# Soft mixture of experts behind linear attention: w2 units 3 and 4 in two loads, six output chunks in a row and their store in two transfers

## The chip and the metric

The kernel runs on one core of one Trainium2 chip. The metric is the time of one execution on the device, in microseconds (us); lower is better.

## What is computed

Linear attention over 8 batches of 8 heads gives a matrix `x` of 4608 tokens by 512, and a soft mixture of 8 experts with 4 slots each works on it:

```python
kv = np.einsum('bhsd,bhse->bhde', k, v)
out = np.einsum('bhsd,bhde->bhse', q, kv)
x = out / sqrt(mean(out * out, -1) + 1e-06) * g_norm      # reshaped to (4608, 512)
...
logits = x @ phi                                           # (4608, 32)
d = softmax of logits over the tokens                      # dispatch
slot_input = (d.T @ x).reshape(E, S_per_e, D)
for e in range(E):
    h = np.maximum(slot_input[e] @ w1[e], 0.0)             # w1[e]: 512 x 1024
    slot_out[e] = h @ w2[e]                                # w2[e]: 1024 x 512
c = softmax of logits over the 32 slots                    # combine
return c @ slot_out                                        # (4608, 512)
```

All of it is float32. The weights are 2 x 8 x 2 MB, the attention's inputs 28 MB, the output 9.4 MB.

## The kernel before

The program is written as one list of operations by hand. A small class (`Order`, with the helper at line 209 that issues all of them) finds out which operation must wait for which and puts a semaphore there; every engine works in the order of the program. So all rows of the profile name line 209, and operations are told apart by their tiles. SBUF is one `arena` of 160 places of 1 KB a partition that inputs, weights and output chunks use one after another; `W_AT` (lines 35 to 39) and `OUT_AT` (line 52) say who lies where.

The first part, to about 113 us, streams k, v and q in, forms the attention's output tile by tile, its norm, the logits and the dispatch sums. Weights follow the inputs on the same queue, SP's; a load waits only until the last reader of its place is done. The rows of `W_ROWS` (lines 40 to 51) are the weights' transfers in the order of the queue; a row with two entries is one transfer.

The second part is the experts. `expert_h(e)` multiplies by w1, `expert_y(e, hf)` by one half (256 columns) of w2: 8 matmuls, 16 passes in float32. The experts from 2 on have w2 in another form: `w2_unit` (line 841) puts the first halves of experts 2 and 3 in unit 2, of 4 and 5 in unit 3, of 6 and 7 in unit 4, and the second halves in units 5, 6 and 7. So the first half of the output columns needs units 0 to 4 only. Unit 3 goes to place 72 and unit 4 behind it to place 88, in one transfer of 128 rows of 32 KB:

```python
    (("w2", 3, None), ("w2", 4, None)),
    (("w2", 5, None), ("w2", 6, None)),
    (("w2", 7, None),),
```

When all first halves are summed, `gather(0)` and `mix(0)` copy and rearrange the result, and `output(0, k, f)` makes chunks 0 to 5 of the output, 768 KB each: matmuls with the combine weights into PSUM, a copy of one half by ACT and of the other by DVE into the arena (chunks 5 and 11 split DVE's half over both). Three PSUM buffers take turns in the first half; the second half has a fourth. Before, four chunks are made, then the second halves of experts 2 to 5, then chunks 4 and 5, then experts 6 and 7, and `gather(1)`, `mix(1)` and chunks 6 to 11 follow. `fill_wide` issues matmuls that nobody reads; two of them stand where PE waits for units 3 and 4 (line 984).

Stores go out when their last chunk is copied. `store_apart` (line 902) sends the odd rows of chunk 0 in four small transfers (two of them from GpSimd) that use a few of the 16 DMA engines each; `store_first` (line 915) sends the even rows of chunks 0 to 2 in one transfer of 64 rows and the odd rows of chunks 1 and 2 in another; then come chunks 3 to 5, 6 and 7, and 8 to 11 in one transfer each (`OUT_ROWS`, line 53).

Of the kernel before, what the change touches and what calls it, by code (L numbers as in the profile page):

```python
# [23 lines left out]
NCH = NT // CT  # L24
NX = 14
EARLY = (5, 1, 0)
LATE_FILL = (4, 3, 3, 1, 1, 2)
TOK = 4608
UNIT = 4096
KB = 256  # L30
# [14 lines left out]
    (("w1", 5, None),),  # L45
    (("w2", 2, 0), ("w1", 6, None)),
    (("w1", 7, None),),
    (("w2", 3, None), ("w2", 4, None)),
    (("w2", 5, None), ("w2", 6, None)),
    (("w2", 7, None),),  # L50
)
OUT_AT = (32, 38, 44, 104, 110, 116, 122, 128, 134, 140, 146, 152)
OUT_ROWS = ((0, 1, 2), (3, 4, 5), (6, 7), (8, 9, 10, 11))
CHUNK = 4 * 12 * 32
APART = (("gpsimd", 0, 26, 2, 1), ("gpsimd", 41, 11, 2, 2), ("sync", 26, 15, 5, 1), ("sync", 52, 12, 3, 1))
STEPS = (7, 6)
# [221 lines left out]
def soft_moe_linear_attention(nc, first_in, kv_in, q0_in, q1_in, kv4_in, kv5_in, t3_in, w_in, out):  # L278
# [37 lines left out]
    def load_w(kind, u, part=None):  # L316
        i = [row[0] for row in W_ROWS].index((kind, u, part))
        lo = sum(row_length(row) for row in W_ROWS[:i])
        n = row_length(W_ROWS[i])
        src = w_in[:, lo * P : (lo + n) * P].rearrange("o (p n) -> (o p) n", p=P)  # L320
        t = homes(kind, u)[part or 0]
        if n > t.shape[-1]:
            t = place(W_AT[kind, u][part or 0], n)
        nc.sync.dma_start(t, src)
# [522 lines left out]
    def expert_h(e):  # L847
        ph = ps.tile([P, 2, 512], F32, tag="m", name=f"ph{e}")[:, 0, :256]
        for c in range(4):
            for j in range(4):  # L850
                nc.tensor.matmul(
                    ph[32 * j : 32 * j + 32],
                    lhsT=sTe[:, (4 * e + c) * NS : (4 * e + c + 1) * NS],
                    rhs=w_block("w1", e, 4 * c + j),
                    start=c == 0,
                    stop=c == 3,
                )
        h = wk.tile([P, 256], F32, tag="part", name=f"h{e}", bufs=3)
        nc.scalar.activation(h, ph, AF.Relu, scale=rs)

        x = xts[(NT - 1 - e // 2) % NX].rearrange("p j n -> p (j n)")
        hTs[e] = x[:, e % 2 * 256 : e % 2 * 256 + 256].rearrange("p (c n) -> p c n", n=NS)
        nc.vector.transpose(out=hTs[e].rearrange("p c n -> p (c n)"), in_=h)
# [51 lines left out]
    def store_first():  # L915
        at = 64 * CHUNK
        for i in range(2):
            n = (3 - i) * CHUNK
            nc.sync.dma_start(out[:, at : at + 64 * n].rearrange("o (m n) -> (o m) n", n=n), place(OUT_AT[i], n)[i::2])
            at += 64 * n  # L920

    def output(hf, k, f):
        z = zs[hf]
        n = (hf * NCH + k) * 2 + f
        at = OUT_AT[n]
        st = place(at, 4 * CT * NS).rearrange("p (a n) -> p a n", a=4)
        shared = n in SHARED
        for v in range(2):
            fourth = hf == 1 and (2 * n + v) % 4 == 3
            apart = shared and v == 1  # L930
            pots = [
                ps.tile([P, 2, 512], F32, tag="y" if y else "m", name=f"po{hf}_{k}_{f}_{v}_{i}", bufs=1 if y else None)
                for i, y in enumerate((False, fourth) if apart else (fourth,))
            ]
            for u in range(2):
                lo = 32 * (2 * v + u)
                po = pots[u if apart else 0]
                nc.tensor.matmul(
                    po[:, 0 if apart else u, : CT * NS].rearrange("p (g x) -> p g x", g=2),
                    lhsT=z[f][lo : lo + 32],  # L940
                    rhs=cT[k][lo : lo + 32],
                    start=True,
                    stop=True,
                )
            if apart:
                nc.vector.tensor_copy(out=st[:, 2], in_=pots[0][:, 0, : CT * NS])
                nc.scalar.copy(st[:, 3], pots[1][:, 0, : CT * NS])
            elif v == 0:
                nc.scalar.copy(st[:, 0:2], pots[0][:, :, : CT * NS])
            else:  # L950
                nc.vector.tensor_copy(out=st[:, 2:4], in_=pots[0][:, :, : CT * NS])
        if n == 0:
            store_apart()
        if n == 2:
            store_first()
        for row in OUT_ROWS[1:]:
            if row[-1] == n:
                lo, m = row[0] * 4 * CT * NS, len(row) * 4 * CT * NS
                nc.sync.dma_start(
                    out[:, lo * P : (lo + m) * P].rearrange("o (p n) -> (o p) n", p=P), place(OUT_AT[row[0]], m)  # L960
                )

    step_over(STEPS[0])
    expert_h(0)
    expert_h(1)
    load_w("w2", 3)
    expert_y(0, 0)
    combine(0)
    expert_h(2)
# [11 lines left out]
    expert_y(3, 0)  # L981
    expert_y(0, 1)
    expert_y(1, 1)
    fill_wide(ps.tile([P, 2, 512], F32, tag="m", name="fill")[:, 0], LATE_FILL[5])
    for e in range(4, NE):
        expert_y(e, 0)
    chunks = [(k, f) for k in range(NCH) for f in range(2)]
    gather(0)
    mix(0)
    output(0, *chunks[0])  # L990
    output(0, *chunks[1])
    output(0, *chunks[2])
    output(0, *chunks[3])
    expert_y(2, 1)
    expert_y(3, 1)
    expert_y(4, 1)
    expert_y(5, 1)
    output(0, *chunks[4])
    output(0, *chunks[5])
    expert_y(6, 1)  # L1000
    expert_y(7, 1)
    gather(1)
# [87 lines left out]
```

## Time and profile before

| | us |
|---|---|
| median of 3 runs | 172.40 (172.13 to 172.85) |
| the profiled execution, its own time | 172.14 |
| its span, from the first to the last instruction | 170.8 |
| PE busy | 150.2 (88%) |
| ACT, DVE, POOL busy | 88.9, 86.0, 59.9 |
| DMA queue of SP | 71.15 MB, 97.6% of 16 engines' span |

The profile covers one execution. A page of it gives busy times and the busy tenths of each engine in 40 slices of the span; a busy PE is one with a matmul in it, whatever that matmul is for. The DMA share of a stretch is the mean over the 16 DMA engines and can pass 1.00 a little, since packets overlap at their ends. "SPq" is SP's queue: its rows give the issue of a transfer, not its run, and the time to landing is counted from the issue to the last of its 16 completions.

### The profile page before, as it was taken

The numbers are of one execution on the slowest core, as the hardware profiler recorded it, in microseconds if no ns is written. First come the engines' busy times: TensorE is split into PE (matmuls) and PEld (weight loads), VectorE is DVE, ScalarE is ACT, GpSimd is POOL, SyncE is SP. The second block draws the span as 40 slices with busy tenths as digits, with TensorE's granted clock in tenths as the row PEclk, the third lists the DMA queues.
The fourth block names the chain that finished last, engine by engine and source line by source line (L and its number), as shares of the span: only waits on it lengthen the run. The fifth ranks groups of instructions, "written<-read, shape, count | busy, mean of one in ns | idle before, by whom it ended". The sixth has DMA issues, their size and how long they took to land.

```text
span 170.8 us, 4512 instructions
## 1 busy us (share of the span) xinstructions
PE 150.2 (88%) x1975; PEld 108.4 (63%) x1975; DVE 86.0 (50%) x184; ACT 88.9 (52%) x230; POOL 59.9 (35%) x72
## 2 busy tenths in 40 slices
PE   7988897989999899999899998999999988989500
PEld 3467776979788888898797785355565453545200
DVE  1122156284677266762946698824888017136600
ACT  3037575796975886859759864202224016146500
POOL 6000708548357745467382679500000004000000
PEclk9999999999999999999999999999999999999955
DMA  5999999999999999999999999999999999999996
GB/s 188 416 433 421 440 421 433 475 415 471 440 410 421 431 440 441 407 403 462 403 453 418 437 405 430 430 435 416 445 453 418 439 410 414 405 426 423 433 437 282
DMA packets 4295, 71.67 MB, mean 420 GB/s; under 512 B 883, under 2 KB 883, under 8 KB 947
## 3 DMA queue, kind: packets, MB, share of 16 engines
q1 hardware_dynamic: 3795, 71.15, 97.6%
q8 instruction: 15, 0.25, 0.5%
q0 software_dynamic: 480, 0.23, 0.5%
q14 instruction: 5, 0.04, 0.1%
HBM read 61.94 MB, written 9.44 MB: 418 GB/s over the span
## 4 chain that ended last, share of the span: by engine, by line
PE 47%; DMA 26%; ACT 12%; DVE 5%; SPq 2%; issue 1%
PE psum L209 47%; DMA arena<-in_kv_dram 13%; DMA arena<-in_w_dram 13%; ACT bd L209 3%; ACT sq L209 3%; ACT xall L209 2%; SPq L209 2%; DVE logits L209 1%; ACT arena L209 1%; DVE ms L209 1%; ACT part L209 1%; ACT d L209 1%; ACT r L209 1%; DVE r L209 0%; DVE d L209 0%
## 5 line engine op out<-in xcount | busy, mean ns | idle before, releaser
L209 PE MATMUL psum<-bd,arena 128*128 128x192 f32 (+1 forms) x320 | 56.1, 335 | 1.9 <-ACT bd L209 1.5
L209 PEld LDWEIGHTS psum<-bd,arena 128*128 128x128 f32 (+1 forms) x320 | 45.4, 179 | 7.1 <-ACT bd L209 2.8
L209 DVE TENSOR_REDUCE ms<-sq 128x16 f32<-128x1024 f32 (+1 forms) x19 | 22.1, 1162 | 33.0 <-ACT sq L209 32.7
L209 POOL TENSOR_TENSOR part<-part,r 128x512 f32<-128x512 f32 x17 | 17.8, 1049 | 49.9 <-DVE r L209 49.9
L209 POOL TENSOR_TENSOR xall<-xall,r 128x512 f32<-128x512 f32 x34 | 34.8, 1044 | 0.0
L209 ACT ACTIVATE sq<-psum 128x512 f32<-128x512 f32 x36 | 21.5, 598 | 12.8 <-PE psum L209 12.6
L209 PE MATMUL psum<-arena 128*64 128x64 f32 (+1 forms) x640 | 21.7, 226 | 2.5 <-DMA arena<-in_kv_dram 2.4
L209 PEld LDWEIGHTS psum<-arena 128*64 128x64 f32 (+1 forms) x640 | 19.0, 137 | 7.4 <-DMA arena<-in_kv_dram 3.7
L209 ACT COPY xall<-psum 128x512 f32<-128x512 f32 x34 | 20.6, 606 | 0.0
L209 ACT COPY part<-psum 128x256 f32<-128x256 f32 (+1 forms) x38 | 13.6, 359 | 9.9 <-DVE part L209 8.8
L209 DVE TENSOR_REDUCE logits<-part 128x64 f32<-128x512 f32 (+1 forms) x18 | 17.8, 988 | 0.0
L209 PE MATMUL psum<-arena,xall 128*32 128x256 f32 x256 | 15.0, 380 | 0.3 <-DMA arena<-in_w_dram 0.3
L209 DVE COPY arena<-psum 128x768 f32<-128x768 f32 (+1 forms) x12 | 10.4, 889 | 8.4 <-PE psum L209 8.4
L209 ACT COPY arena<-psum 128x768 f32<-128x768 f32 (+1 forms) x14 | 10.1, 755 | 8.3 <-PE psum L209 8.3
L209 PE MATMUL psum<-logits,part 32*128 32x384 f32 x96 | 12.8, 521 | 1.5 <-ACT arena L209 0.9
L209 POOL DMA_DIRECT2D out_dram<-arena x2 | 1.5, 730 | 33.3 <-ACT arena L209 33.3
L209 PE MATMUL psum<-arena,sq 128*32 128x256 f32 x224 | 12.7, 379 | 0.2 <-DVE sq L209 0.2
L209 PEld LDWEIGHTS psum<-arena,xall 128*32 128x32 f32 x256 | 8.0, 110 | 7.3 <-DMA arena<-in_w_dram 1.8
L209 PE MATMUL psum<-xall,d 128*32 128x129 f32 x288 | 10.8, 278 | 0.8 <-ACT d L209 0.8
L209 ACT COPY bd<-psum 64x128 f32<-64x128 f32 (+1 forms) x32 | 9.9, 308 | 1.6 <-PE psum L209 1.4
L209 PEld LDWEIGHTS psum<-logits,part 32*128 32x128 f32 x96 | 6.1, 183 | 7.1 <-ACT arena L209 4.2
L209 PEld LDWEIGHTS psum<-arena,sq 128*32 128x32 f32 x224 | 7.2, 110 | 5.2 <-DVE sq L209 0.6
(76 smaller groups left out, 128.6 us busy)
## 6 DMA issues: line engine op xcount, KB each, us to landing
arena<-in_w_dram SPq DMA_DIRECT2D x5, 4096.0 KB, 22.4
arena<-in_t_dram SPq DMA_DIRECT2D x1, 6912.0 KB, 36.0
arena<-in_w_dram SPq DMA_DIRECT2D x2, 3072.0 KB, 22.5
arena<-in_kv_dram SPq DMA_DIRECT2D x2, 2304.0 KB, 23.7
arena<-in_kv_dram SPq DMA_DIRECT2D x1, 4608.0 KB, 42.8
arena<-in_w_dram SPq DMA_DIRECT2D x2, 2048.0 KB, 24.1
arena<-in_kv_dram SPq DMA_DIRECT2D x1, 3584.0 KB, 32.4
arena<-in_kv_dram SPq DMA_DIRECT2D x3, 1152.0 KB, 13.2
```

The source lines that it names most:

```text
L209: inst = getattr(engine, method)(*args, **kwargs)
```

## The change

The loads of w2 units 3 and 4 are two transfers of 2048 KB instead of one of 4096 KB; unit 3 is issued behind `expert_h(0)` and unit 4 behind `expert_h(1)`, where the two were issued together. Chunks 0 to 5 are made one after another; the second halves of experts 2 to 5 come behind them. The two fill matmuls ahead of experts 4 to 7 go, and one stands ahead of the second half of expert 6. The chunks lie at places 72 to 108 and 108 to 144 in one piece, and `store_first` sends the even rows of all six chunks (64 rows of 36 KB) and the odd rows of chunks 1 to 5 (64 rows of 30 KB) when chunk 5 is done; the transfer of chunks 3 to 5 goes. The odd rows of chunk 0 are sent as before. The last part of the diff, on the host's rearranging of the output, is left out here.

```diff
--- before.py
+++ after.py
@@ -24,7 +24,7 @@
 NCH = NT // CT
 NX = 14
 EARLY = (5, 1, 0)
-LATE_FILL = (4, 3, 3, 1, 1, 2)
+LATE_FILL = (4, 3, 3, 1, 1, 1)
 TOK = 4608
 UNIT = 4096
 KB = 256
@@ -45,12 +45,13 @@
     (("w1", 5, None),),
     (("w2", 2, 0), ("w1", 6, None)),
     (("w1", 7, None),),
-    (("w2", 3, None), ("w2", 4, None)),
+    (("w2", 3, None),),
+    (("w2", 4, None),),
     (("w2", 5, None), ("w2", 6, None)),
     (("w2", 7, None),),
 )
-OUT_AT = (32, 38, 44, 104, 110, 116, 122, 128, 134, 140, 146, 152)
-OUT_ROWS = ((0, 1, 2), (3, 4, 5), (6, 7), (8, 9, 10, 11))
+OUT_AT = tuple(range(72, 144, 6))
+OUT_ROWS = ((0, 1, 2, 3, 4, 5), (6, 7), (8, 9, 10, 11))
 CHUNK = 4 * 12 * 32
 APART = (("gpsimd", 0, 26, 2, 1), ("gpsimd", 41, 11, 2, 2), ("sync", 26, 15, 5, 1), ("sync", 52, 12, 3, 1))
 STEPS = (7, 6)
@@ -915,7 +916,7 @@
     def store_first():
         at = 64 * CHUNK
         for i in range(2):
-            n = (3 - i) * CHUNK
+            n = (len(OUT_ROWS[0]) - i) * CHUNK
             nc.sync.dma_start(out[:, at : at + 64 * n].rearrange("o (m n) -> (o m) n", n=n), place(OUT_AT[i], n)[i::2])
             at += 64 * n
 
@@ -951,7 +952,7 @@
                 nc.vector.tensor_copy(out=st[:, 2:4], in_=pots[0][:, :, : CT * NS])
         if n == 0:
             store_apart()
-        if n == 2:
+        if n == OUT_ROWS[0][-1]:
             store_first()
         for row in OUT_ROWS[1:]:
             if row[-1] == n:
@@ -962,8 +963,9 @@
 
     step_over(STEPS[0])
     expert_h(0)
+    load_w("w2", 3)
     expert_h(1)
-    load_w("w2", 3)
+    load_w("w2", 4)
     expert_y(0, 0)
     combine(0)
     expert_h(2)
@@ -981,22 +983,16 @@
     expert_y(3, 0)
     expert_y(0, 1)
     expert_y(1, 1)
-    fill_wide(ps.tile([P, 2, 512], F32, tag="m", name="fill")[:, 0], LATE_FILL[5])
     for e in range(4, NE):
         expert_y(e, 0)
     chunks = [(k, f) for k in range(NCH) for f in range(2)]
     gather(0)
     mix(0)
-    output(0, *chunks[0])
-    output(0, *chunks[1])
-    output(0, *chunks[2])
-    output(0, *chunks[3])
-    expert_y(2, 1)
-    expert_y(3, 1)
-    expert_y(4, 1)
-    expert_y(5, 1)
-    output(0, *chunks[4])
-    output(0, *chunks[5])
+    for k, f in chunks:
+        output(0, k, f)
+    for e in range(2, 6):
+        expert_y(e, 1)
+    fill_wide(ps.tile([P, 2, 512], F32, tag="m", name="fill")[:, 0], LATE_FILL[5])
     expert_y(6, 1)
     expert_y(7, 1)
     gather(1)
...
```

On SP, the end of its order (w_dram are the weights, out_dram the output). Before:

```order
L209 DMA xall<-in_w_dram 128x4096
L209 DMA arena<-in_w_dram 128x8192 x2
L209 DMA arena<-in_w_dram 128x4096
L209 DMA out_dram<-arena 5x3x1536
L209 DMA out_dram<-arena 3x4x1536
L209 DMA out_dram<-arena 64x4608
L209 DMA out_dram<-arena 64x3072
L209 DMA out_dram<-arena 128x4608
L209 DMA out_dram<-arena 128x3072
L209 DMA out_dram<-arena 128x6144
```

After:

```order
L210 DMA xall<-in_w_dram 128x4096
L210 DMA arena<-in_w_dram 128x4096 x2
L210 DMA arena<-in_w_dram 128x8192
L210 DMA arena<-in_w_dram 128x4096
L210 DMA out_dram<-arena 5x3x1536
L210 DMA out_dram<-arena 3x4x1536
L210 DMA out_dram<-arena 64x9216
L210 DMA out_dram<-arena 64x7680
L210 DMA out_dram<-arena 128x3072
L210 DMA out_dram<-arena 128x6144
```

The 128x8192 load of units 3 and 4 became two of 128x4096, and the stores of 64x4608, 64x3072 and 128x4608 became one of 64x9216 and one of 64x7680.

On PE, the end of its order: `arena,xall` are w2 and the experts' hidden values (32 rows are four experts' halves, 16 are two), `ones` the fill, `part,sel` the rearranging, `logits,part` the chunks (4 a chunk). Before:

```order
L209 MATMUL psum<-xall,sq 32x256 x16
L209 MATMUL psum<-arena,xall 32x256 x32
L209 MATMUL psum<-ones 128x512 x2
L209 MATMUL psum<-arena,xall 32x256 x32
L209 MATMUL psum<-part,sel 128x128 x2
L209 MATMUL psum<-logits,part 128x384 x16
L209 MATMUL psum<-arena,xall 32x256 x32
L209 MATMUL psum<-logits,part 128x384 x8
L209 MATMUL psum<-arena,xall 32x256 x16
L209 MATMUL psum<-part,sel 128x128 x2
L209 MATMUL psum<-logits,part 128x384 x24
```

After:

```order
L210 MATMUL psum<-xall,sq 32x256 x16
L210 MATMUL psum<-arena,xall 32x256 x64
L210 MATMUL psum<-part,sel 128x128 x2
L210 MATMUL psum<-logits,part 128x384 x24
L210 MATMUL psum<-arena,xall 32x256 x32
L210 MATMUL psum<-ones 128x512
L210 MATMUL psum<-arena,xall 32x256 x16
L210 MATMUL psum<-part,sel 128x128 x2
L210 MATMUL psum<-logits,part 128x384 x24
```

The fills between the first halves are gone, so 64 rows of experts stand in one piece; the 16 and 8 matmuls of chunks 0 to 3 and 4 to 5 became 24 in a row, ahead of the second halves of experts 2 to 5; one fill stands behind these.

## Rows read from the trace of the kernel before

**Rows 1.** The page: busy engines, DMA busy tenths in 40 slices, the hardware queue (packets, MB, share).

```profile
PE 150.2 (88%) x1975; PEld 108.4 (63%) x1975; DVE 86.0 (50%) x184; ACT 88.9 (52%) x230; POOL 59.9 (35%) x72
...
DMA  5999999999999999999999999999999999999996
...
q1 hardware_dynamic: 3795, 71.15, 97.6%
```

**Rows 2.** Stretches (from:to us): length, busy us by engine, granted PE clock, DMA share, GB/s.

```profile
3.00:60.00 57.00, 52.27 (x664) 42.88 (x665) 25.18 (x54) 36.17 (x99) 25.24 (x27) 1.00 1.02 434
60.00:100.00 40.00, 39.13 (x551) 33.23 (x552) 25.45 (x55) 31.28 (x88) 22.39 (x23) 1.00 0.99 426
140.00:144.00 4.00, 3.39 (x28) 1.68 (x29) 2.38 (x3) 2.32 (x4) 1.73 (x3) 1.00 0.94 401
150.00:152.00 2.00, 1.97 (x24) 1.09 (x28) 0.75 (x2) 1.16 (x2) 0.00 (x0) 1.00 0.95 395
160.00:164.00 4.00, 0.66 (x4) 0.04 (x2) 0.79 (x2) 0.87 (x2) 0.00 (x0) 0.89 1.01 433
168.00:171.00 3.00, 0.00 (x0) 0.00 (x0) 0.00 (x0) 0.00 (x0) 0.00 (x0) 0.50 0.52 221
```

**Rows 3.** The chain that ended last: start us, us, what.

```profile
122.38 22.20 DMA arena<-in_w_dram
...
144.62 4.53 PE psum L209 x72
...
160.71 0.54 DVE arena L209
```

**Rows 4.** Timeline of SP, one window for each issue: start us, us, queue, line, operation.

```profile
117.20 0.33 SPq L209 DMA_DIRECT2D arena<-in_w_dram  x1
122.38 0.33 SPq L209 DMA_DIRECT2D arena<-in_w_dram  x1
125.83 0.33 SPq L209 DMA_DIRECT2D arena<-in_w_dram  x1
144.43 0.54 SPq L209 DMA_DIRECT2D out_dram<-arena  x1
151.70 0.36 SPq L209 DMA_DIRECT2D out_dram<-arena  x1
161.32 0.33 SPq L209 DMA_DIRECT2D out_dram<-arena  x1
```

**Rows 5.** DMA issues in the windows of 117.20, 122.38, 125.83, 161.32: KB, us to landing.

```profile
arena<-in_w_dram SPq DMA_DIRECT2D x1, 4096.0 KB, 17.6
arena<-in_w_dram SPq DMA_DIRECT2D x1, 4096.0 KB, 22.2
arena<-in_w_dram SPq DMA_DIRECT2D x1, 2048.0 KB, 23.6
out_dram<-arena SPq DMA_DIRECT2D x1, 3072.0 KB, 9.3
```

**Rows 6.** Timeline of PE: start us, us, operation, count, idle before it and its releaser.

```profile
132.61 1.98 PE L209 MATMUL psum<-ones 128*128 128x512 f32 x4
...
134.86 3.66 PE L209 MATMUL psum<-arena,xall 128*32 128x256 f32 x64 [0.27 <-DMA arena<-in_w_dram]
...
151.09 1.93 PE L209 MATMUL psum<-arena,xall 128*32 128x256 f32 x32
```

**Rows 7.** Timeline of ACT and DVE: the copies of chunks 0, 1 and 2, 3, 4, 5.

```profile
140.77 1.50 ACT L209 COPY arena<-psum 128x768 f32<-128x768 f32 x2 [0.74 <-PE psum L209]
...
142.58 1.82 DVE L209 COPY arena<-psum 128x768 f32<-128x768 f32 x2 [0.80 <-PE psum L209]
...
144.55 0.80 ACT L209 COPY arena<-psum 128x768 f32<-128x768 f32 x1 [0.95 <-PE psum L209]
...
149.24 0.96 DVE L209 COPY arena<-psum 128x768 f32<-128x768 f32 x1 [3.66 <-PE psum L209]
...
151.19 0.48 ACT L209 COPY arena<-psum 128x384 f32<-128x384 f32 x1 [0.52 <-PE psum L209]
```

More of the change, by code (lines that the diff above doesn't have):

```diff
@@ L1074 @@
     n = 4 * CT * NS
-    three = np.empty((P, 3 * n), np.float32)
+    some = np.empty((P, len(OUT_ROWS[0]), n), np.float32)
     at = 0
@@ L1079 @@
             w = n // c
-            three[p, h * w : h * w + w] = res[0, at : at + w]
+            some[p, 0, h * w : h * w + w] = res[0, at : at + w]
             at += w
-    three[::2] = res[0, at : at + 192 * n].reshape(64, 3 * n)
-    three[1::2, n:] = res[0, at + 192 * n : 3 * P * n].reshape(64, 2 * n)
-    chunks = [three[:, k * n : k * n + n] for k in range(3)]
+    for i in range(2):
+        part = some[i::2, i:]
+        part[...] = res[0, at : at + part.size].reshape(part.shape)
+        at += part.size
+    chunks = [some[:, k] for k in range(some.shape[1])]
     for row in OUT_ROWS[1:]:
```

## The prediction

> **What bounds the kernel.** I read four views. The page first: PE is busy for 88% of the span, but the 16 DMA engines are busy for nine tenths or more in every slice between the first and the last, and nearly all bytes go through one hardware queue, SP's [rows 1]. The stretches come second, because a share over the span may hide a hole: the DMA share is 1.02 and 0.99 over the two long stretches of loads, at 434 and 426 GB/s; it is 0.94 from 140 to 144 us, 0.95 from 150 to 152, and 1.01 from 160 to 164, where PE is nearly done [rows 2]. So the kernel moves a fixed number of bytes at a fixed rate. In the last 30 us the stretches below 1.00 hold 4 x 0.06 + 2 x 0.05 = 0.34 us of missing transfer, and the last three microseconds are the queue's end, 0.52.
>
> The third view, the chain that ended last, names the same thing for one place and another for the rest: the w2 transfer issued at 122.38 is waited for until 144.58, then PE and the copies carry the chain to 161.25 [rows 3], when the last store is made ready. It is issued at 161.32 [rows 4] and lands 9.3 us later [rows 5], at 170.62 of a span of 170.8. Its 3072 KB (3.15 MB) take 7.3 us at 430 GB/s, so 2.0 us are left for its start, for waiting behind the store before it and for its end. The share of 1.01 from 160 to 164 says that the queue was still full when it came, or nearly so. So two chains end within about a microsecond of each other: the queue, which sets the time, and the chain of chunks, just ahead of it.
>
> **The change, part by part.** *The load of w2 units 3 and 4.* Today it is one transfer of 4096 KB, issued at 117.20 [rows 4] and landed 17.6 us later [rows 5], at 134.80. PE stands from the end of two fills until 134.86 and then runs the first halves of experts 4 to 7: 64 passes, 3.66 us, with 0.27 us of idle time put down to the load [rows 6]. After the change unit 3 is a transfer of its own, ahead of unit 4. The next pair of loads gives the rate at the same place of the queue: units 5 and 6 land at 122.38 + 22.2 = 144.58, unit 7 (2048 KB) at 125.83 + 23.6 = 149.43, 4.85 us later [rows 4, 5]. So unit 3 should land at about 134.80 - 4.85 = 129.95 and unit 4 at 134.80 as before. Experts 4 and 5 need unit 3 alone; they start at 132.61, where the two fills stood (1.98 us, gone from here), and take 3.66 / 2 = 1.83 us, to 134.44. Experts 6 and 7 wait to 134.86 and end at 136.69 instead of 138.52. **The first half is ready 1.83 us earlier.** PE's gap shrinks to 0.42 us, today it is 0.27 us; its granted clock is 1.00 (the level of 2.4 GHz) in all stretches to 152 us [rows 2], and I charge nothing. The extra issue costs SP 0.33 us [rows 4] while SP is idle, and the load comes no earlier on the DMA engines, since they are busy without a hole: nothing.
>
> The Trainium skill speaks against this edit: "DMA: Bandwidth & Descriptors", in "Anatomy of one DMA", puts a fixed cost of about 2.0 us on each DMA, and its "Rules for kernel authors" want transfers joined. By that the estimate would be unit 4 at 136.8 and the first half only where it was. The rows on the loads say otherwise where transfers follow each other: 2048 KB in 4.85 us is 432 GB/s, the rate of the long stretches, with nothing left over.
>
> *Six chunks in a row.* Today chunk 0's first copy starts at 140.77 and chunk 3's at 144.55 [rows 7], so three chunks take 3.78 us with three PSUM buffers. After the change chunk 3's first copy starts at 144.55 - 1.83 = 142.72. Chunk 4's vector copy follows it as chunk 1's follows chunk 0's: 142.58 + 0.96 + 3.78 - 1.83 = 145.49 is its end (0.96 from the row of a single copy). Chunk 5 is shared between two engines at its end: today its last piece on ACT ends at 151.19 + 0.48 = 151.67, 1.47 us behind the end of chunk 4's vector copy at 149.24 + 0.96 = 150.20 [rows 7]. So chunk 5 is done at 146.96 and **the even rows are issued at about 147.0**, where today the store of chunks 0 to 2 is issued at 144.43 and that of chunks 3 to 5 at 151.70 [rows 4]. The first 1920 KB come 2.6 us later than today, the next 2304 KB 4.7 us earlier.
>
> *Do the DMA engines go empty in between?* All stores are 12 x 768 = 9216 KB (9.44 MB), 21.95 us at 430 GB/s. They end at 170.62, so the average engine passes from loads to stores at 148.67. The 384 KB of odd rows of chunk 0 come first, 0.91 us; their issue moves ahead with the first half. So the average engine wants the even rows at 148.67 + 0.91 = 149.6. What lies between an issue and its first bytes isn't shown; it is bounded by the 0.33 us of the issue itself [rows 4] and the 2.0 us left over at the last store, which hold its end and its waiting too. I take the harsh end, being the nearest row of a store: 147.0 + 2.0 = 149.0, still 0.6 us ahead of the average engine. Engines ahead of the average may stand still for some tenths or a microsecond; those are the ones that stand still today at 150 to 152 us. I take 0 for the time, with 0 to +0.4 us as bounds. In return the hole at 150 to 152 should close: 0.1 us, on engines that were ahead anyway, so 0 again.
>
> *Eight larger packets for sixteen.* The stores are one transfer fewer, the loads one more: SP's number of issues stays as it was, and the bytes too.
>
> *The second half.* PE goes on to experts 2 to 5, second halves, just before chunk 5's last ACT piece, as experts 6 and 7 do today (151.09 against 151.19 [rows 6, 7]). That piece starts at 146.96 - 0.48 = 146.48, so they start at 146.4; units 5 and 6 landed at 144.58, so no wait. 3.66 us bring it to 150.0; then comes the fill that was moved here, half of 1.98 = 0.99 us, to 151.0; unit 7 has landed at 149.43. Experts 6 and 7 take 1.93 us [rows 6], to 152.95 instead of 153.02. **The second half, and with it the last store's issue, moves by -0.1 us.** What the first half gained is spent on the six chunks in one go, which are paced by the copies (8.4 us instead of 4.8 + 2.9), and on the fill, which had cost nothing in the wait for units 3 and 4.
>
> **The sum.** Queue: same bytes, same rate, 0 (bounds -0.3 to +0.4). Last store: -0.1, off the path by the share of 1.01. So 172.1 us against the profiled execution's own 172.14 (span 170.8 and 1.3 around it). The median of the three runs is 172.40, 0.26 above it. I forecast **172.3 us**, no change that a measurement of this kernel can tell (which is about 0.5%, 0.86 us).
>
> **The rivals.**
> *The store gate (slower).* Everything but the 384 KB now waits for chunk 5. With the issue at T, the end is T + 2.0 + 21.0 (8832 KB at 430 GB/s) at the harsh bound; that passes 170.62 from T = 147.6 on. The mechanism decides if the first half doesn't come 1.83 us earlier, or the six chunks run slower than 1.26 us each. With nothing gained T is 148.8, the end 171.8, the time 173.4; with the mild bound of 0.33 us it is 172.1 still. For it: one store holds all, and PE, ACT and DVE alternate on three buffers. Against: 0.6 us of margin at the harsh bound. Chance 0.17, of which 0.10 above +0.5%.
> *A split load lands late.* If each transfer had 2.0 us of its own also behind another, as the last store's remainder would allow, unit 4 would land at 136.8 and T be 148.8 or more: 173.4 at the harsh bound. Against it stands the 4.85 us of unit 7. The rule that says so is the one of "DMA: Bandwidth & Descriptors" above. Chance 0.03, half of it above +0.5%.
> *The chain of chunks is the bound, and the holes close (faster).* If the last store is really gated by chunk 11, and the 0.34 us of holes close and the engines end more evenly (the last stretch does 0.52 x 3 = 1.56 us of work in 2.6 us), up to 0.1 + 0.34 + 0.5 = 0.9 us go: 171.2. Against: the share of 1.01 up to 164 us, and the last store moves by 0.1 only. Chance 0.20, of which 0.12 below -0.5%.
> *The change does nothing*: PE waits for units 3 and 4 together. It isn't so in the order of PE, where experts 4 and 6 have a load each to wait for; what it would cost is the store gate's 173.4.
>
> **How the numbers follow.** The forecast has 0.60 (171.8 to 172.8: the bounds of the queue and the scatter of the runs, 172.13 to 172.85); the gate 0.17, the late load 0.03, the faster case 0.20. Faster by over 0.5%: 0.12. Slower: 0.10 + 0.01 = 0.11. Within: 0.77. The range takes in the forecast's and most of both sides: 171.4 to 173.2 us.
>
> **What would show it.** Right: PE starts experts 4 and 5 at about 132.6 and the chunks at about 138.0; the even rows are issued near 147.0; the DMA share from 150 to 152 rises to 1.00; the last store is issued near 161.2 and lands near 170.6. Wrong: a DMA share below 0.9 between 146 and 150 us with the last store landing later (the gate); unit 4 later than 135.5 (the late load); the last store landing less than 8 us after its issue with an end below 170 (the chain of chunks).

## The result, and the profile after

The changed kernel takes **173.34 us** (median of six runs, 173.28 to 173.63); the kernel before, on the same chip, 172.38 (six runs, 172.13 to 172.85). The ratio is **1.0063 [1.0048, 1.0079]**: slower by 0.96 us, and outside the forecast's range (171.4 to 173.2). Some executions, here and below, take over 1.5% longer than the fastest of the same kernel; the ratios leave those out. The profiled execution took 173.33 us with a span of 172.0, 1.2 us longer than before's. A repeat of the same kernel gave 173.38 and 1.0066 (further below).

The page of the changed kernel, the lines that answer to [rows 1], and one more, the queue that carries TensorE's instructions:

```profile
PE 150.1 (87%) x1973; PEld 108.4 (63%) x1973; DVE 85.9 (50%) x184; ACT 89.0 (52%) x230; POOL 59.9 (35%) x72
...
DMA  5999999999999999999999999999999999999994
...
q1 hardware_dynamic: 3795, 71.15, 97.0%
q8 instruction: 15, 0.25, 0.5%
```

Packets and bytes are those of [rows 1], and so is the work but for one fill matmul; only the last slice is emptier. The stretches after (columns as in [rows 2]; a packet's whole time is booked where it starts, so short stretches scatter about 1.00):

```profile
140.00:144.00 4.00, 3.47 (x26) 1.55 (x26) 2.99 (x4) 2.45 (x5) 2.04 (x3) 1.00 0.97 410
144.00:146.00 2.00, 1.79 (x11) 0.84 (x11) 1.20 (x3) 1.53 (x2) 0.00 (x0) 1.00 0.97 404
146.00:147.00 1.00, 1.00 (x10) 0.37 (x14) 0.31 (x1) 0.15 (x1) 0.00 (x0) 1.00 0.96 394
147.00:148.00 1.00, 1.00 (x24) 0.63 (x20) 0.00 (x0) 0.32 (x1) 0.00 (x0) 1.00 0.87 345
150.00:152.00 2.00, 2.00 (x22) 0.71 (x18) 0.00 (x0) 0.00 (x0) 0.00 (x0) 1.00 1.09 461
160.00:164.00 4.00, 0.92 (x4) 0.30 (x4) 1.09 (x2) 1.17 (x2) 0.00 (x0) 0.88 1.05 449
168.00:171.00 3.00, 0.00 (x0) 0.00 (x0) 0.00 (x0) 0.00 (x0) 0.00 (x0) 0.50 0.57 246
```

Against [rows 2] the hole at 150 to 152 us is closed (1.09 for 0.95), a small one stands at 147 to 148 (0.87), and the queue's end is later. The issues on SP's queue, one window for each:

```profile
115.53 0.33 SPq L210 DMA_DIRECT2D arena<-in_w_dram  x1
117.26 0.33 SPq L210 DMA_DIRECT2D arena<-in_w_dram  x1
147.35 0.54 SPq L210 DMA_DIRECT2D out_dram<-arena  x1
161.62 0.35 SPq L210 DMA_DIRECT2D out_dram<-arena  x1
```

and how long after its issue each lands:

```profile
arena<-in_w_dram SPq DMA_DIRECT2D x1, 2048.0 KB, 14.6
arena<-in_w_dram SPq DMA_DIRECT2D x1, 2048.0 KB, 17.7
out_dram<-arena SPq DMA_DIRECT2D x1, 2304.0 KB, 9.1
out_dram<-arena SPq DMA_DIRECT2D x1, 3072.0 KB, 10.2
```

Unit 3 lands at 115.53 + 14.6 = 130.1, unit 4 at 117.26 + 17.7 = 135.0, the even rows are issued at 147.35, all nearly as forecast. The last store is issued 0.30 us later than before [rows 4] but takes 10.2 us instead of 9.3 [rows 5]: it lands at 171.8 instead of 170.6. Where these 0.9 us are shows in the last stretches, first of the changed kernel, then of the kernel before:

```profile
169.00:169.50 0.50, 0.00 (x0) 0.00 (x0) 0.00 (x0) 0.00 (x0) 0.00 (x0) 0.50 0.80 344
169.50:170.00 0.50, 0.00 (x0) 0.00 (x0) 0.00 (x0) 0.00 (x0) 0.00 (x0) 0.50 0.24 98
170.00:170.50 0.50, 0.00 (x0) 0.00 (x0) 0.00 (x0) 0.00 (x0) 0.00 (x0) 0.50 0.12 49
```

```profile
169.00:169.50 0.50, 0.00 (x0) 0.00 (x0) 0.00 (x0) 0.00 (x0) 0.00 (x0) 0.50 0.69 295
169.50:170.00 0.50, 0.00 (x0) 0.00 (x0) 0.00 (x0) 0.00 (x0) 0.00 (x0) 0.50 0.01 0
170.00:170.50 0.50, 0.00 (x0) 0.00 (x0) 0.00 (x0) 0.00 (x0) 0.00 (x0) 0.50 0.00 0
```

A share of 0.12 of 0.5 us and 16 engines is 0.96 us of one engine: the time of **one packet, on one DMA engine**, that starts after 170.0 (49 GB/s for 0.5 us are its 24 KB), when in the kernel before no engine starts any after 169.5. The mean hides it. The trace's records of single packets (start, length, bytes) show when each engine's last packet is done: fifteen engines end at 169.77 to 170.46 us, the sixteenth at 171.40. In the kernel before, all sixteen end at 169.46 to 170.33.

The DMA queues in a window of 1.5 us tell what that engine may have had besides. The changed kernel, 153 to 154.5 us, and the kernel before, 151 to 152.5 (packets, MB, share of 16 engines; q8 carries instructions):

```profile
q1 hardware_dynamic: 26, 0.61, 96.9%
q8 instruction: 1, 0.02, 3.7%
```

```profile
q1 hardware_dynamic: 57, 0.54, 86.4%
q8 instruction: 1, 0.02, 4.1%
```

One packet of queue q8 lies in each: 0.037 x 1.5 x 16 = 0.89 us of one engine, and 0.98 us before. It is an instruction fetch of TensorE (the runs below show it: their count follows the number of TensorE's instructions). There are 15 in a run, one for about every 263 of PE's and PEld's 3946 rows, 0.25 MB together. The Trainium skill ("Runtime: NRT & Kernel Launch", "Terms") says that an engine's instruction memory is refilled in blocks of 16 KiB; 0.25 MB in 15 packets agrees. The Trainium skill ("DMA: Bandwidth & Descriptors", "Queues, rings and completion order") has a DMA engine alternate between queues packet by packet; that fits a fetch between two packets of a store. The views show no engine for a packet; the packet records do, further below.

So the theory to test, **the fetch behind the hold**: the even rows' hold until 147.35 lets engines that were ahead stand still and lose their lead; the fetch at 153 then costs one of them 0.9 us or more that nothing makes up. Its rivals: **the hold alone** (a later store is a later end), **the size of packets** (36 KB packets for 18 KB), **the last store's issue** (161.62 for 161.32), and **the load in two**. The expectations call these theories by letters and say with each what they stand for.

### The profile page after: what moved, and what is told of

Same layout as the page of the kernel before. It is cut to its first block, busy times and chain, and to the rows that moved or that the text cites. A ratio compares the mean times of both kernels' runs of the same rounds, so it can differ in the third digit from the quotient of the medians.

```text
span 172.0 us, 4507 instructions
## 1 busy us (share of the span) xinstructions
PE 150.1 (87%) x1973; PEld 108.4 (63%) x1973; DVE 85.9 (50%) x184; ACT 89.0 (52%) x230; POOL 59.9 (35%) x72
## 4 chain that ended last, share of the span: by engine, by line
PE 48%; DMA 24%; ACT 12%; DVE 7%; SPq 2%; issue 1%
PE psum L210 48%; DMA arena<-in_kv_dram 13%; DMA arena<-in_w_dram 10%; ACT bd L210 3%; ACT sq L210 3%; ACT xall L210 2%; SPq L210 2%; DVE arena L210 1%; DVE logits L210 1%; ACT arena L210 1%; DVE ms L210 1%; ACT part L210 1%; ACT d L210 1%; DVE part L210 1%; ACT r L210 1%
## 5 line engine op out<-in xcount | busy, mean ns | idle before, releaser
L210 PE MATMUL psum<-logits,part 32*128 32x384 f32 x96 | 13.5, 524 | 1.5 <-ACT arena L210 0.7
L210 ACT COPY arena<-psum 128x768 f32<-128x768 f32 (+1 forms) x14 | 10.2, 754 | 5.3 <-PE psum L210 5.2
```

The lines of the kernel that those rows point to most:

```text
L210: inst = getattr(engine, method)(*args, **kwargs)
```

## Experiments on the hold and the other parts

Times are medians; each ratio is against runs of the kernel before on the same chip.

**The store of three chunks back**, the rest of the change kept (even rows of chunks 0 to 2 are issued at 142.90):

```diff
-OUT_ROWS = ((0, 1, 2, 3, 4, 5), (6, 7), (8, 9, 10, 11))
+OUT_ROWS = ((0, 1, 2), (3, 4, 5), (6, 7), (8, 9, 10, 11))
```

> The changed kernel with its six chunks in a row and its two loads, but with the stores cut as before: the even rows of chunks 0 to 2 are issued behind chunk 2 (about 143), chunks 3 to 5 behind chunk 5 (about 147.4). Theory G (the gate: engines that are through with their loads stand still from about 146 to 148.6 us, and the one that still has an instruction fetch of PE's ahead of it, 0.9 us and more, then ends last): no engine stands still, 172.2 us (172.0 to 172.5). Theory P (the 36 KB and 30 KB packets cost, by themselves or by holding up that fetch): packets are small again, 172.3 as well. Theory C (the last store, issued 0.3 us later than before, sets the end): unchanged, 173.3.

Measured: 172.37 us (172.04 to 173.51, 12 runs), 1.0015 [0.9989, 1.0042]. The loss is gone, so it lies in the store. Three of the twelve runs, those with a mean granted clock of 0.965 or 0.966, are at 173.2 to 173.5; the others at 172.0 to 172.5. The clock comes back below.

**A hold with small packets, first try**, the same with `if n == 5: store_first()`:

> As e1, with the small packets (18 and 12 KB), but nothing of the even rows is issued before chunk 5 is done, as in the changed kernel. Tells the gate from the packets. G: 173.2 us (172.9 to 173.5). P: 172.3 to 172.6. C: 173.3.

Measured: 172.23 us, 1.0011 [0.9994, 1.0028]. A miss: the store was issued at 142.84, since its rows are complete after chunk 2 and nothing holds it there. It repeats the run above and says nothing of packets.

**A hold with small packets**, with the store put behind that of chunks 3 to 5, which does wait (issues at 147.66, 148.08 and 148.66):

```diff
-        if n == OUT_ROWS[0][-1]:
-            store_first()
...
+        if n == 5:
+            store_first()
```

> A mended e2, whose store of chunks 0 to 2 was not held at all (its issue stood at 142.84). The changed kernel with the packets of before (18 KB and 12 KB), in the order chunks 3 to 5, even rows of 0 to 2, odd rows of 1 and 2, so that all of them wait for chunk 5 (about 147.3). Theory G (standing still until 148.6 on an engine that has PE's last instruction fetch still ahead): that engine still ends late, only the fetch costs 1.4 us instead of 1.9 beside small packets: 0.4 to 0.9 us over before, a ratio of 1.003 to 1.005. Theory P (large packets, by themselves or by what the fetch costs beside them, without the hold): ratio 1.000. The changed kernel itself has 1.006.

Measured: 173.08 us (172.86 to 173.53), 1.0045 [1.0023, 1.0066]. The seven runs with a mean clock of 0.971 or more are at 172.86 to 173.08, the five at 0.965 at 173.21 to 173.53, against 172.25 of the kernel before. So some 0.7 us of the loss are back with 18 and 12 KB packets: most of it isn't their size. The trace is of the run at 173.53, in which the second halves of experts 2 to 5 took 5.09 us for 3.66 and all sixteen engines end together, at 171.50 to 171.64; it shows nothing of the fetch.

**Large packets without a hold**: chunks 3 to 5 lie elsewhere and are not stored, old contents go out in their stead, and the store of six is issued at chunk 2, 142.78 us:

```diff
-OUT_AT = tuple(range(72, 144, 6))
+OUT_AT = (72, 78, 84, 32, 38, 44) + tuple(range(108, 144, 6))
...
-        if n == OUT_ROWS[0][-1]:
+        if n == 2:
```

> The opposite of e7: packets of 36 KB and 30 KB, but issued behind chunk 2 (about 142.9). Chunks 3 to 5 are put elsewhere and not stored; their part of the rows that are sent holds old contents, so that part of the output is something else. Theory G: no engine stands still, ratio 1.000 (0.998 to 1.002). Theory P: the late fetch costs 1.9 us again, ratio 1.003 to 1.006. If both hold and half is added by each, e7 and e9 lie between 1.002 and 1.004.

Measured: 172.28 us (171.86 to 173.45; the four runs above 173 have a mean clock of 0.965 or 0.966), 1.0012 [0.9982, 1.0042]. Large packets are free when they are issued early, and so is a fetch, which this run has at 153.0 us.

**Half the hold**, five chunks in the first store, the sixth by itself (`OUT_ROWS = ((0, 1, 2, 3, 4), (5,), (6, 7), (8, 9, 10, 11))`):

> Even rows leave as chunks 0 to 4 together at about 146.0 us, chunk 5 by itself at about 147.3. Theory A (one engine has only about 1 us to spare between its dry spell and the end once the fetch is on it): a store 1.3 us earlier fills most of it again, ratio 1.000 to 1.003. Theory C (any store of most even rows in one transfer is late by its size, not by its hour): ratio 1.005 or more.

Measured: 172.43 us, 1.0023 [1.0004, 1.0042]. The store is issued at 145.56, 1.8 us earlier than in the changed kernel, and most of the loss is gone.

**The load in two, alone**: the kernel before with units 3 and 4 in two transfers and without the two fills.

> The kernel before with nothing but the load of units 3 and 4 in two transfers and without the two fills ahead of experts 4 to 7. The first half comes 1.5 us earlier, chunks 0 to 3 and the first store too. The split's own cost, if it has one, would show here: G and P say none, ratio 1.000 (0.998 to 1.002), since the queue sets the time and nothing is held. If a further transfer costs: above 1.004.

Measured: 172.28 us, 1.0008 [0.9984, 1.0032]. The second transfer costs nothing, and a first half that is ready earlier brings nothing.

**The load in one, in the changed kernel** (`(("w2", 3, None), ("w2", 4, None))` again, everything else kept):

> The changed kernel with units 3 and 4 in one transfer again, so that the first half is ready later by the 1.5 us that the split gained, and the even rows are issued at about 148.9. G: the engines stand still for 1.5 us more, all of them now, 174.7 us (174.3 to 175.2). P: unchanged by that, 173.3. C: the second half moves by 1.5 us too and with it the last store, 174.8; e8 (no fill) will tell C.

Measured: 175.85 us (175.09 to 176.86, 4 runs), 1.0204 [1.0166, 1.0241]. With the first half late, the hold lasts to 150.90 and all DMA engines run dry. These stretches of it show that TensorE's clock fell too:

```profile
135.00:139.00 4.00, 4.00 (x48) 2.58 (x51) 0.00 (x0) 0.00 (x0) 0.00 (x0) 0.61 1.02 442
148.00:150.00 2.00, 1.79 (x8) 0.56 (x4) 1.42 (x2) 0.80 (x1) 0.00 (x0) 0.88 0.38 130
150.00:152.00 2.00, 2.00 (x19) 0.80 (x22) 0.00 (x0) 0.48 (x1) 0.00 (x0) 0.50 0.03 12
```

This is the store gate as the prediction described it, at a hold that is 3.5 us longer, with the clock's share in it not told apart.

**No fill before experts 6 and 7** (`LATE_FILL` ends in 0):

> The changed kernel without the fill ahead of the second half of expert 6: the second half and the last store come 1.0 us earlier (last issue about 160.6 instead of 161.62). Theory C (the last store sets the end): ratio to before 1.000 to 1.001. G and P (an engine's own queue sets it): unchanged, 1.005 to 1.007.

Measured: the last store is issued at 160.19, 1.4 us earlier, and the time is 173.28 us, 1.0058 [1.0038, 1.0077]. One packet still starts after 170 us (the share from 170.0 to 170.5 is 0.12 again). The last store's issue is not the bound.

## Experiments on the fetch

The number of instructions decides when a fetch comes. So a fetch can be moved by instructions that stand elsewhere and do nothing.

**Without a late fetch**: the second halves of experts 2 to 7 and some of the k-v products are left out, six more fills stand in place of the halves, the hold stays (issue at 147.25). The last store is issued at 160.54, 1.1 us earlier, which by the run without a fill is worth nothing:

```diff
-            for c in range(4):
+            for c in (0, 2, 3) if self.b in (2, 3) else range(4):
...
-    for e in range(2, 6):
-        expert_y(e, 1)
-    fill_wide(ps.tile([P, 2, 512], F32, tag="m", name="fill")[:, 0], LATE_FILL[5])
-    expert_y(6, 1)
-    expert_y(7, 1)
+    fill_wide(ps.tile([P, 2, 512], F32, tag="m", name="fill")[:, 0], 4 + LATE_FILL[5] + 2)
```

> The changed kernel with the second halves of experts 2 to 7 left out and six fills of the same length in their place, and two batches' second quarter of the k-v products left out: 230 instructions of PE fewer, so that the last instruction fetch (at 153 us) has no reason any more and the one before it falls ahead of the store. The gate stays at 147.35. G with the fetch: the last engine loses 1.3 us or so of its lateness, 172.3 us (172.1 to 172.6). G by the standing still alone: 173.3. P by the packets alone: 173.3; P by the fetch: 172.3. Computes something else in the second half of the columns.

Measured: 172.22 us (171.97 to 172.58), **0.9998 [0.9978, 1.0018]**. With the hold, the store of six and the large packets all in place, the loss is gone. But work is missing too; two controls follow.

**First control**, 48 narrow fp32 matmuls in that place, so that the count is kept:

> The second halves of experts 2 to 7 are replaced by 48 narrow fp32 matmuls of 64 columns whose results go nowhere (so the output of the last batches is not the reference's), which keeps the number of TensorE instructions, and with it the instruction fetch at about 153 us, while TensorE has as little to do as in the run that left these instructions out (0.9998). Theory A (the hold of all even rows together with the late fetch on one DMA engine): ratio 1.004 to 1.008, with one DMA engine ending about 1 us behind the others. Theory B (that run gained by an earlier last store or by less work on TensorE): ratio 0.998 to 1.002.

Measured: 185.68 us, and nothing on the theories. The matmuls meant as padding were slow, and the granted clock was 0.50 from 148 to 160 us, while they ran (the row holds the 96 passes of the narrow ones and two of the fill):

```profile
146.46 18.33 PE L210 MATMUL psum<-ones 128*128 128x64 f32 x98
```

**Second control**, the run without a late fetch, with more and shorter fills far ahead, at 105 to 111 us:

```diff
-    fill_wide(ps.tile([P, 512], F32, tag="m", name="fill"), LATE_FILL[0])
+    late = ps.tile([P, 512], F32, tag="m", name="fill")
+    for i in range(64):
+        n = 128
+        nc.tensor.matmul(late[:, :n], lhsT=zeros[:, :P], rhs=zeros[:, :n], start=True, stop=True)
...
-    fill(LATE_FILL[1], home=tail_ps[:, 1], cols=512)
+    fill(2 * LATE_FILL[1], home=tail_ps[:, 1], cols=256)
...
-    fill(LATE_FILL[2], home=tail_ps[:, 1], cols=512)
+    fill(2 * LATE_FILL[2], home=tail_ps[:, 1], cols=256)
```

> The run without second halves of experts 2 to 7 and without some products of k and v (it leaves that work out, so its output is not the reference's; 0.9998) with some 124 TensorE instructions more in the fills at 105 to 111 us, 64 short bf16 matmuls, so that the next instruction fetch, which that run did not reach, comes at 155 to 157 us behind the hold. Everything from 113 us on is as in that run. Theory A (hold and a fetch behind it): ratio 1.004 to 1.009 again, one DMA engine about 1 us behind. Theory B (that run gained by its missing work): 0.998 to 1.002.

Measured: 173.32 us (173.2 to 174.09, 6 runs), **1.0069 [1.0046, 1.0092]**. From 113 us on the two runs have the same instructions, and their stores are issued within 0.04 us of each other (even rows 147.25 and 147.22, last store 160.54 and 160.50); one has a fetch more. Its window from 158 to 161 us:

```profile
q1 hardware_dynamic: 99, 1.08, 85.1%
q8 instruction: 1, 0.02, 1.8%
```

0.018 x 3 x 16 = 0.86 us. From 146 us to the end the run without has no row for q8 at all. The stretches from 170.0 to 170.5, first without, then with the fetch:

```profile
170.00:170.50 0.50, 0.00 (x0) 0.00 (x0) 0.00 (x0) 0.00 (x0) 0.00 (x0) 0.50 0.01 0
```

```profile
170.00:170.50 0.50, 0.00 (x0) 0.00 (x0) 0.00 (x0) 0.00 (x0) 0.00 (x0) 0.50 0.12 49
```

The one packet after 170.0 comes and goes with the fetch. With the hold in place, **the fetch is the microsecond**. And at 153 us the hold is needed for it: the large packets issued early bear a fetch at 153.0 us without a loss.

**The engine of the fetch.** The packet records of the trace don't name engines, but they chain up to sixteen of them: on a full queue a packet starts some 4 ns before the one ahead of it on its engine ends, and 15 ns before where that one is a fetch. From the even rows on, each chain of the changed kernel has the same 24 store packets. The chain with the fetch at 153.28 us is the one that ends last, at 171.40. So it is in the repeat (171.20, the others to 170.42), without the fill (171.16, to 170.39) and in the second control (171.25, to 170.49).

The fetch costs its engine more than its own 0.88 us: the store packet ahead of it took 1.96 us and the one behind it 1.78, where 173 of the run's 192 packets of that size took 1.36. Together that is 1.9 us. With the large packets issued early it was 0.95, and 0.37 more on the packet behind it, 1.3 us.

The lead is what the hold takes away: with the early issue the engines start on the even rows between 146.75 and 149.06 us, in the changed kernel none before 148.55 and the last at 149.54. The engine of the fetch is among the first, 1.0 us ahead of the last one, and has 1.9 us to pay: it ends 0.9 us behind.

**A late fetch in the kernel before**, which has no hold: the same edit with 60 matmuls of 256 and 128 columns in turn, so that a sixteenth fetch comes near 159 us:

> The kernel before, with its store of three chunks and no hold, and some 116 more TensorE instructions in the fills at 105 to 111 us, so that the fifteenth fetch comes at about 146 us and a sixteenth at 160 to 163. Theory A, in its wider form (a fetch behind the point where engines last stand still comes on top of the queue's time of its engine, in any kernel): ratio 1.004 to 1.009, one DMA engine about 1 us behind the others. Theory A in its narrow form (it takes the hold as well): 0.999 to 1.003.

Measured: 173.62 us (173.25 to 173.94, 11 runs), **1.0073 [1.0048, 1.0097]**. The page has the sixteenth fetch, the window from 158 to 161 us has it (0.025 x 3 x 16 = 1.2 us), and packets start in both last stretches, where the kernel before has none. But the edit did more than add a fetch: the loads of w2 units 3 and 4 are issued 1.3 us later (118.51 for 117.20) and the last store 0.85 us later (162.17 for 161.32). Fourteen engines end at 170.31 to 170.43, the two others at 171.35 and 171.69, and only one of these two can have had the fetch.

```profile
q8 instruction: 16, 0.26, 0.5%
```

```profile
q8 instruction: 1, 0.02, 2.5%
```

```profile
170.00:170.50 0.50, 0.00 (x0) 0.00 (x0) 0.00 (x0) 0.00 (x0) 0.00 (x0) 0.50 0.13 49
170.50:171.00 0.50, 0.00 (x0) 0.00 (x0) 0.00 (x0) 0.00 (x0) 0.00 (x0) 0.50 0.11 49
```

**Its control**, with 36 matmuls: 15 fetches, none after 149 us.

> The kernel before with 68 more TensorE instructions in the fills at 105 to 111 us in place of 116: the fifteenth fetch moves from 151.3 to about 147 us and no sixteenth comes. If the sixteenth fetch is what cost the run with 116 its 0.7%, this one is at 0.998 to 1.002; if the added matmuls themselves cost something (later weights, later stores), 1.003 to 1.007.

Measured: 172.25 us (171.89 to 173.18), **1.0006 [0.9990, 1.0023]**. These 36 matmuls cost nothing, but they leave the loads where they were (117.25) and the last store too (161.31). So the pair doesn't tell the sixteenth fetch from the later loads, and whether a late fetch costs its time without a hold isn't shown. What is shown: without a hold the kernel before bears a fetch at 151.3 us and the large packets one at 153.0; with it the changed kernel doesn't bear the one at 153.3.

**The fetch of the changed kernel moved into the hold.** Three tries. First by 21 narrow matmuls in place of one wide fill at the very start:

> The changed kernel with some 80 more TensorE instructions in the first 7 us (21 narrow matmuls that nobody reads in place of one wide one, about as long as it), so that the last instruction fetch is asked for at about 147.8 us in place of 151, while the even rows are held and engines stand still. Everything behind is as in the changed kernel. Theory A (the fetch falls on an engine that had lost its lead in the hold): the fetch now fills time that is empty anyway, ratio 0.999 to 1.003. Theory B (the fetch is nothing; the hold, or the size of the packets, costs the microsecond): 1.005 to 1.008.

Measured: 172.64 us (172.12 to 177.07, 13 runs), 1.0033 [1.0015, 1.0052], between the theories. Then with 33 of them, for one fetch more:

> As the run before, with some 128 more TensorE instructions: the fetch is asked for at about 146 us, and one more, the sixteenth, at about 157, behind the hold. Theory A: the added one costs its engine what the one at 153 us did, and that engine has nothing left to fill: ratio 1.004 to 1.010. Theory B: 1.005 to 1.008, as with any hour of the fetch. The pair tells: if the first of the two is near 1.000 and this one above 1.004, the hour of the fetch decides, since the added work is nearly the same.

Measured: 176.48 us, 1.0225 [1.0193, 1.0257], far above either. Neither tells: the fills at the start took 8.85 us in the second of them, for 3.31 in the changed kernel, and TensorE never made up for it (even rows at 149.29); the trace of the first is of its run at 177.07 us, with the even rows at 152.43. Next, with the fills at 105 to 111 us (44 of the short matmuls):

> The changed kernel with the fill at 104.7 us (8 passes, 3.7 us) made of 44 short bf16 matmuls and the two fills of three at 108.7 and 109.8 us of six half as wide: some 84 more TensorE instructions, in about the same time, so that the last instruction fetch is asked for at about 148 us, while the even rows are held (issue 147.3 to 147.6), in place of 151. Theory A (hour of the fetch): ratio 0.998 to 1.003, all 16 DMA engines ending within 0.5 us. Theory B (the hold or the size of the packets costs the microsecond, whatever the fetch): 1.005 to 1.008, one engine 1 us behind. Between 1.003 and 1.005 both have a share.

Measured: 173.38 us, 1.0083 [1.0051, 1.0114]. The fetch moved to 147.6, but a sixteenth came at 164.3, inside the last store. In its profiled run (174.89 us) no packet starts from 171.5 to 172.0 (0.01) and one after 172.0 (0.11): one engine alone at the end again. Last with 36, which stays below the sixteenth:

> As the run with 84 more TensorE instructions at 105 to 111 us, with 68 in place of 84 (36 short matmuls for 44), so that no sixteenth instruction fetch comes by the end and the fifteenth is asked for at about 148 us, within the hold. Theory A (the hour of the fetch): ratio 0.999 to 1.003, no DMA engine more than 0.6 us behind the others at the end. Theory B (the hold or the size of the packets by itself): 1.005 to 1.008.

Measured: 173.04 us (172.25 to 173.36, 12 runs), 1.0039 [1.0015, 1.0063]. No engine ends alone in its profiled run (the share is 0.80 from 170.5 to 171.0 and 0.01 after 171.0), yet that run took 173.36 us, for another reason:

```profile
146.00:148.00 2.00, 2.00 (x14) 0.73 (x18) 0.26 (x1) 0.48 (x1) 0.00 (x0) 0.64 0.87 350
148.00:150.00 2.00, 2.00 (x24) 0.98 (x20) 0.00 (x0) 0.00 (x0) 0.00 (x0) 0.50 1.19 467
```

```profile
146.74 5.24 PE L210 MATMUL psum<-arena,xall 128*32 128x256 f32 x64
```

The clock fell to 0.50, the level of 1.2 GHz, just after the six chunks, and the second halves of experts 2 to 5 took 5.24 us for 3.66. The last store was ready 1.6 us later. The five runs with a mean clock of 0.965 to 0.967 are at 173.1 to 173.4, the seven others at 172.25 to 173.3. The median of the seven is 172.97, still 0.84 us above the kernel before: moving the fetch into the hold takes off little, and the fall of the clock puts something on in some runs.

**The changed kernel again**, for this clock:

> The changed kernel as it is, for comparison on the same chip: ratio 1.005 to 1.008 by every theory; if its runs fall into two groups by their mean granted clock, the group with the lower clock is above the other by 0.2 to 0.4 us only, and both are above the kernel before.

Measured: 173.38 us (173.14 to 173.42, 5 runs), 1.0066 [1.0053, 1.0079]. Runs with the mean clock at 0.974 to 0.980 take 173.14 to 173.38, those at 0.966 and 0.970 173.38 and 173.42. In the changed kernel the clock is not the loss; where the fetch isn't in the way, as with the store of three, runs with the lower clock take some 1.2 us more (173.2 to 173.5 against 172.0 to 172.5).

## Why the prediction was wrong

**The queue is the bound: right.** Bytes, packets and rate are as before, and the time went where the queue ends. No version beat the kernel before; the best stands at 0.9998.

**The load: right.** Unit 4 lands at 134.98 (forecast 134.80), unit 3 at 130.1 (129.95). The load in two alone is 1.0008. The fixed cost of about 2.0 us for each DMA, which the prediction set against the rows, doesn't show here; the rows were right to be taken. The Trainium skill ("DMA: Bandwidth & Descriptors", "Anatomy of one DMA") fits it to transfers issued from GpSimd, and its rule on joining ("Rules for kernel authors") speaks of many small ones; these are SP's, of 2048 KB.

**The first half earlier: right, smaller.** PE runs experts 4 and 5 ahead of unit 4, so the rival that the change does nothing is out. PE's idle time before experts 6 and 7 is 0.65 us (forecast 0.42), and the first copy comes at 139.29, 1.48 us earlier for 1.83. PE's rows of the changed kernel (start, us, operation, idle time before it and its releaser):

```profile
135.12 1.93 PE L210 MATMUL psum<-arena,xall 128*32 128x256 f32 x32 [0.65 <-DMA arena<-in_w_dram]
...
140.14 1.62 PE L210 MATMUL psum<-logits,part 32*128 32x384 f32 x12 [0.25 <-ACT arena L210]
142.11 3.58 PE L210 MATMUL psum<-logits,part 32*128 32x384 f32 x22 [0.36 <-DVE arena L210]
145.90 0.91 PE L210 MATMUL psum<-logits,part 32*128 32x384 f32 x2 [0.20 <-DVE arena L210]
146.74 3.66 PE L210 MATMUL psum<-arena,xall 128*32 128x256 f32 x64
150.33 1.12 PE L210 MATMUL psum<-ones 128*128 128x512 f32 x2
151.38 1.93 PE L210 MATMUL psum<-arena,xall 128*32 128x256 f32 x32
```

**Six chunks and the hour of the store: right.** 147.35 for 147.0, before the hour of 147.6 at which the gate was to decide.

**The second half: off by 0.4 us, without effect.** The last store is issued at 161.62 for 161.2, most of it the 0.35 us by which the first half fell short. An issue 1.4 us earlier changed nothing (1.0058).

**The step that failed** is the one on the DMA engines: "Engines ahead of the average may stand still for some tenths or a microsecond; those are the ones that stand still today at 150 to 152 us. I take 0 for the time, with 0 to +0.4 us as bounds." The sum was made for the average engine, which did have its data in time. The time is the last engine's: one of those ahead still had a fetch of instructions to run, which cost it 1.9 us, and the hold had left it a lead of 1.0 us. The term measured +0.96 us. Queue q8 stood on the page of the kernel before (15 packets, 0.5%) and is in no term of the sum. Half a percent of sixteen engines is little; of one engine's last 20 us, 1.9 us are 9%.

The margin of 0.6 us was too large as well: the sum took 170.62, the landing of the last store, for the end of the average engine, but the sixteen engines of the kernel before end at 169.84 on average. So the average engine wanted the even rows at 148.8 and not at 149.6. Their first packets start at 148.55, 1.2 us after the issue, between the two bounds of 0.33 and 2.0 us.

**The rivals.** The store gate came nearest: engines wait for the held store and the end is later. Its price was wrong: it was worked out for the average engine, with nothing below an issue at 147.6 us, and has no fetch in it. Its sign, a share below 0.9 between 146 and 150 us with the last store landing later, shows only as 0.87 in the one microsecond from 147, with a landing 1.2 us later. The late load and the faster case fell with their runs: neither the closed hole nor an earlier first half gave time back.

**The clock** was charged with nothing because it was 1.00 in all rows. That held for the profiled run of the changed kernel but not for all runs of its kin: in several of them it was lower, and in three traces (a clock of 0.58 to 0.65 from 146 to 148 us) it fell at the end of the six chunks. The Trainium skill ("TensorE: Matmul & The Clock Gate", "A second HAM failure mode: psum-queue depth-cycling") tells, for another kernel with bf16 groups of 512 columns, of a clock that changes level when PE idles briefly and often between groups that take turns on PSUM. PE's pauses of 0.20 to 0.36 us, in which it waits for copies at 140 to 146 us, agree with it; but the run shown above has them too and kept 1.00, so why only some runs fall isn't shown.

**What stays open.** Why the store packet ahead of the fetch is long too (1.96 us for 1.36) in the changed kernel, and not where the large packets are issued early. Whether a late fetch costs time without a hold. And the runs with the fetch moved into the hold spread from 172.25 to 173.3 even where the mean clock is 0.973 or more: the one trace of them is of a run with the lower clock, so what those runs lose isn't shown.

## What to carry to other kernels

Where a queue of stores sets the end, do its sum for the engine that ends last, not for the mean: look for a last stretch with a share of one sixteenth or two, and for what else that engine carries. A store that is held until more of it is ready takes away the lead that covers such things. In this kernel stores issued early cost nothing, in small packets or large, and fewer, larger transfers gave no time back. And when an edit changes the number of instructions, see where the last instruction fetches fall.

## What the runs showed of the hardware

- TensorE's instructions come through the same 16 DMA engines as the data, 0.86 to 1.2 us of one engine for each late fetch, and 1.3 to 1.9 us with what its neighbours among the store packets take longer. With the stores held, one fetch at 159 us of 171 is the difference between 0.9998 and 1.0069. The fifteenth fetch came with 1919 matmuls on the page and not with 1857, the sixteenth with 2015 and not with 2013.
- Narrow fp32 matmuls are no cheap padding: 66 passes of 64 columns and two of 512 took 8.85 us at a granted clock of 1.00, where 44 bf16 matmuls of 256 and 128 columns took 3.80 us at 1.00:

```profile
104.67 3.80 PE L210 MATMUL psum<-zeros 128*128 128x256 bf16 x44
```

- A load split in two on a full queue costs nothing that can be measured: 1.0008 [0.9984, 1.0032].
